# Attention, GLU and routed experts on one core: a new order for the first pass over the GLU's weights

## The chip, the core and the metric

The kernel runs on one core of one Trainium2 chip. Five engines work side by side, each through its own list of instructions in program order: TensorE (PE, matrix products), VectorE (DVE), ScalarE (ACT), GpSimd (POOL) and SyncE (SP), which here only issues DMAs. The tile framework puts semaphores where one engine needs another's result; it does not reorder. An instruction that waits holds back all that stands behind it on its engine. The metric is the device time of one execution in microseconds (us). Execution times come from several runs; the profile is of one execution.

## What is computed

Sizes: 2304 tokens (4 sequences of 576), 8 heads of 64, width 512. A sliding window attention, a GLU with 1536 inner columns and a mixture of eight experts with two per token follow each other.

```python
# attention: position i sees i-63 .. i of its own sequence
scores = scale * q @ k.T;  masked outside the window;  attn = softmax(scores);  x = attn @ v
# GLU; its three weights are float64
gate = 1.0 / (1.0 + np.exp(-(x @ w_gate)))
x = ((gate * (x @ w_val)) @ w_out).astype(np.float32)
# experts
noisy_logits = x @ w_gate2 + np.log1p(np.exp(x @ w_noise)) * noise
top2 = np.argpartition(-noisy_logits, 2, axis=1)[:, :2]      # softmax over the two
for e in range(8):
    out[mask] += top2_w[mask, k, None] * (np.maximum(x[mask] @ w1[e], 0.0) @ w2[e])
```

## The kernel before

Tokens go in 18 tiles of 128; three tiles make a block (384 columns), six blocks a pass each over the GLU's weights (NB = 6). The weights come in twelve words f of 128 inner columns (NF1 = 12), each with three parts: gate, val and out. A product in near single precision is made of three matmuls with split operands, high x high, high x low and low x high (`mm3`, lines 56 to 58).

**A step** is one f of one block: 12 matmuls for gate and 12 for val (128x384, `glu_in`), tanh on ACT (L313), the product on DVE (`mul`, L318), its split into a high half on ACT (`gh`, L325) and a low half on DVE (`low`, L329), and 9 matmuls of 128x512 with the part out of the step before (`out`). One bank each holds gate and val, so the next step's val waits for `mul`.

**Conversion.** The weights arrive as float64, in pairs of 32-bit words, 512 KB for a part. In the first pass each step f also converts word f + 2, in seven instructions on 1536 columns: ACT takes the magnitude from the upper word (`m`, L182) and the rounding from the lower (`r`, L190); DVE shifts (`s`, L195), puts in the sign (`o`, L200) and adds the rounding (`a`, L206); ACT writes the high half (`h`, L214), DVE the low half (`l`, L219) in the step after. The magnitude of word f + 3 is begun in step f. Raw and converted word share one place per f, tag `W{f}`. The magnitude is held by turns in a buffer of its own (`mA`) and in the first half of the place of word 11 (`mB`); the rounding lies in that place's second half. So raw word 11 can only be loaded when word 10 has been rounded. The places of words 8 to 10 hold the queries, keys, values and scores of attention tiles 1 and 2 first; raw 8 to 10 are loaded after steps 1 to 3, raw 11 after step 8.

**Attention** of one tile spreads over four steps: scores (`S`, PE), mask and minimum (`M`, eight custom instructions on DVE, L246), exponential (`E`, ACT, L253), reciprocal (`R`) and normalisation in two halves (`N0`, `N1`, L264) on DVE, transposes in two halves of four (`PT0`, `PT1`, PE, L270), product with v (`O`), split of the result (`X`, L297).

**What sets the order.** The framework keeps the order in which the code is written. For the steps it is given by four strings, ORDER for the first pass and ORDER1 for the others, one string for each of four consecutive steps (f % 4). The prologue, before the steps, is written out by hand: attention of tiles 0 to 2 and the conversion of words 0 and 1. SP's queue takes all loads of that part: qk and v tiles, raw words, the noise (2304 lines of 32 bytes) and an initial fill of the table `slots`.

**Later.** In passes 1 to 5 the routing is worked in; then each of the eight experts gathers up to 640 rows by five indirect DMAs on POOL (L649), and adds its results into the output by five more (L720). `slots` is written by 36 indirect DMAs (L498).

The strings, and the loads that a step may issue:

```python
ORDER = (
    "l r gate M2 E2 s tanh val M3 E3 o mul gh m a low h out",
    "l r gate E4 s tanh val R o mul gh N0 m a low h out N1",
    "PT0 l r gate PT1 s tanh val o mul gh m a low h out",
    "O S X l r gate M0 E0 s tanh val o mul M1 E1 gh m a lv lq low h out",
)
if b == 0 and f in (1, 2, 3, 8):
    load_raw(f + 7 if f < 4 else 11)
```

Of the kernel before, what the change touches and what calls it, by code (L numbers as in the profile page):

```python
# [19 lines left out]
P = 128  # L20
# [25 lines left out]
def build(nc, tc, a, out):  # L46
# [80 lines left out]
    with c1:  # L127
# [6 lines left out]
        def place(f, dt, name):  # L134
# [24 lines left out]
        def load_raw(f, js=range(3)):  # L159
            for i in js:  # L160
                if f < NF1:
                    if f not in WR:
                        r = place(f, I32, "raw")
                        WR[f] = r.rearrange("p (n w) -> p n w", w=2)
                    nc.sync.dma_start(WR[f][:, i * 512:(i + 1) * 512].rearrange("p n w -> p (n w)"),
                                      a["moe_w"].bitcast(I32)[f, i])
# [13 lines left out]
        def cv_m(f, i=W3):  # L180
            if f < NF1:
                nc.scalar.activation(cv_ms(f)[:, cut(i)].bitcast(F32), WR[f][:, cut(i), 1].bitcast(F32), AF.Abs,  # L182
                                     scale=2.0 ** -112)

        def cv_r(f, i=W3):
            if f < NF1:
                if f not in rnd:
                    r = pr.tile([P, 3 * 512], I32, tag="x2", name="rnd")
                    rnd[f] = r
                nc.scalar.activation(rnd[f][:, cut(i)], WR[f][:, cut(i), 0].bitcast(U32), AF.Copy, scale=2.0 ** -29)  # L190

        def cv_s(f, i=W3):
            if f < NF1:
                m = cv_ms(f)[:, cut(i)]
                nc.vector.tensor_scalar(m, m, 3, None, op0=OP.logical_shift_left)  # L195

        def cv_o(f, i=W3):
            if f < NF1:
                m = cv_ms(f)[:, cut(i)]
                nc.vector.scalar_tensor_tensor(m, WR[f][:, cut(i), 1], -2147483648, m, op0=OP.bitwise_and,  # L200
                                               op1=OP.bitwise_or)

        def cv_a(f, i=W3):
            if f < NF1:
                m = cv_ms(f)[:, cut(i)]
                nc.vector.tensor_tensor(m, m, rnd[f][:, cut(i)], op=OP.add)  # L206

        def cv_h(f, i=W3):
            if f < NF1:
                m = cv_ms(f)[:, cut(i)].bitcast(F32).rearrange("p (i c) -> p i c", c=512)  # L210
                if f not in WP:
                    w = place(f, F32R, "W")
                    WP[f] = w.rearrange("p (i a c) -> p i a c", i=3, a=2)
                nc.scalar.activation(WP[f][:, i, 0], m, AF.Copy)  # L214

        def cv_l(f, i=W3):
            if f < NF1:
                m = cv_ms(f)[:, cut(i)].bitcast(F32).rearrange("p (i c) -> p i c", c=512)
                nc.vector.tensor_tensor(WP[f][:, i, 1], m, WP[f][:, i, 0].bitcast(F32), op=OP.subtract)  # L219
# [30 lines left out]
        def attn_E(t, cs):  # L250
            sm, st = Pt[t]
            for c in cs:
# [48 lines left out]
        def glu_in(b, f, i, cols=slice(0, BW), ks=range(NK)):  # L301
# [4 lines left out]
            h, l = WP[f][:, i, 0], WP[f][:, i, 1]  # L306
# [27 lines left out]
        def glu_out(b, f):  # L334
# [3 lines left out]
            h, l = WP[f][:, 2, 0], WP[f][:, 2, 1]  # L338
# [168 lines left out]
        def fill_slots():  # L507
            fill = pr.tile([P, NS, 4], I32, tag="x2", name="fill")
# [18 lines left out]
        for rs in (slice(0, 1), slice(1, 4)):  # L527
            nc.sync.dma_start(qk0[:, rs], a["qk"][0, :, rs])
        load_raw(0, (0,))
        load_vv(0)  # L530
        load_qk(1)
# [4 lines left out]
        load_raw(1)  # L536
        attn_S(0, SB[0])
        load_qk(3)
        load_raw(2)
        attn_M(0, LO)  # L540
        attn_E(0, LO)
        late_consts()
        attn_M(0, HI)
        attn_E(0, range(4, 7))
# [17 lines left out]
        attn_X(0)  # L562
        load_vv(3)
        load_raw(3)
        load_raw(4)
        attn_E(1, HI)
        cv_a(0)
        nrm(1, 0)
        cv_h(0)
        pts(1, 0)  # L570
        attn_M(2, range(8))
        attn_E(2, LO)
# [136 lines left out]
        def y_out(e, j):  # L709
# [42 lines left out]
        )  # L752
        ORDER1 = (
# [250 lines left out]
```

## Time and profile before

| | us |
|---|---|
| median of three runs | 1067.2 (1065.19 to 1068.86) |
| the profiled execution, its own time | 1065.99 |
| its span | 1064.2, at a mean granted clock of 0.985 |
| PE busy | 1007.4 (95%) |
| DVE, ACT, POOL busy | 576.6, 385.6, 153.5 |

The page cuts the span into 40 slices; in the first seven PE is busy for four to eight tenths, after that for nine or more. The first pass ends with the last product out of step 11, which starts at 159.26 us. [...] A wait is listed under the engine that waited, with what came last. In timelines the brackets hold the idle time just ahead of an instruction and its releaser. "DVE early" or "DVE m" is the scratch that the conversion works in.

### The profile page before, as it was taken

What the parts mean: (1) busy time and instruction counts of PE and PEld (TensorE: products, weight loads), DVE (VectorE), ACT (ScalarE), POOL (GpSimd) and SP (SyncE); (2) the same over time, 40 slices, a digit from 0 to 9 for tenths busy, and PEclk for the clock granted to TensorE, in tenths of its full rate; (3) what the DMA queues carried; (4) which work ended last, traced back from release to release, by engine and by line L of the source; (5) the groups of instructions that cost most, each with busy time, mean ns of one, the idle gap of its engine ahead of it and who ended that gap; (6) DMA issues with size and microseconds to landing.
All of it is one profiled execution on the core that took longest, in us unless ns stands there. A gap on an engine that the chain in (4) does not pass through costs nothing.

```text
span 1064.2 us, 16667 instructions
## 1 busy us (share of the span) xinstructions
PE 1007.4 (95%) x6460; PEld 918.2 (86%) x6460; DVE 576.6 (54%) x1594; ACT 385.6 (36%) x868; POOL 153.5 (14%) x210
## 2 busy tenths in 40 slices
PE   4787789999999999999999999999999999999995
PEld 3776679999999999999998889999999999999994
DVE  6788747776766776776333634343434344334331
ACT  5767533223233333332113233233333333333321
POOL 0000000000200200020221224022130505050302
PEclk9988989999999999999999999999999999999998
DMA  9860223222223333342704435434362717262403
GB/s 338 316 260 1 104 85 115 104 94 86 83 102 114 94 108 104 104 108 82 259 2 138 151 119 114 144 73 146 89 170 80 179 59 162 78 158 101 88 2 53
DMA packets 56568, 126.78 MB, mean 119 GB/s; under 512 B 13968, under 2 KB 14112, under 8 KB 56480
## 3 DMA queue, kind: packets, MB, share of 16 engines
q1 hardware_dynamic: 46304, 104.56, 29.0%
q0 software_dynamic: 10176, 21.07, 10.1%
q8 instruction: 53, 0.87, 0.3%
q14 instruction: 35, 0.29, 0.1%
HBM read 101.11 MB, written 24.49 MB: 118 GB/s over the span
## 4 chain that ended last, share of the span: by engine, by line
PE 81%; issue 6%; DVE 4%; DMA 3%; ACT 3%; POOL 1%; SPq 0%; DVEq 0%; ACTq 0%; POOLq 0%
PE gv L56 9%; PE gv L58 9%; PE gv L57 9%; PE hp L57 6%; PE hp L56 6%; PE hp L58 6%; PE yacc L56 6%; PE yacc L57 6%; PE yacc L58 6%; PE acc L56 4%; PE acc L58 4%; PE acc L57 4%; PE PTp L270 2%; PE xgp L662 2%; PE Sp L232 1%
## 5 line engine op out<-in xcount | busy, mean ns | idle before, releaser
L56 PE MATMUL gv<-xT,W 128*128 128x384 f32 (+2 forms) x584 | 204.2, 350 | 3.0 <-ACT th L313 2.3
L57 PE MATMUL gv<-xT,W 128*128 128x384 f32 (+2 forms) x584 | 198.4, 340 | 0.0
L58 PE MATMUL gv<-xT,W 128*128 128x384 f32 (+2 forms) x584 | 198.4, 340 | 0.0
L687 DVE SCALAR_TENSOR_TENSOR hl<-hp,hh 128x320 fp32r<-128x320 f32 (+2 forms) x128 | 62.9, 491 | 198.7 <-ACT hh L686 194.9
L56 PE MATMUL hp<-xgT,h 128*128 128x320 f32 (+2 forms) x512 | 162.3, 317 | 0.0
L58 PE MATMUL hp<-xgT,l 128*128 128x320 f32 (+2 forms) x512 | 159.5, 312 | 0.0
L57 PE MATMUL hp<-xgT,h 128*128 128x320 f32 (+2 forms) x512 | 159.4, 311 | 0.0
L686 ACT ACTIVATE hh<-hp 128x320 fp32r<-128x320 f32 (+2 forms) x128 | 56.0, 438 | 218.7 <-PE hp L58 218.7
L396 DVE CUSTOM_DVE_ANT_0 dump<-x,wb 128x512 bf16<-128x512 f32 x192 | 132.1, 688 | 3.1
L56 PE MATMUL yacc<-h,hh 128*128 128x512 f32 (+1 forms) x328 | 126.9, 387 | 0.0
L57 PE MATMUL yacc<-l,hh 128*128 128x512 f32 (+1 forms) x328 | 126.6, 386 | 0.0
L58 PE MATMUL yacc<-h,hl 128*128 128x512 f32 (+1 forms) x328 | 126.5, 386 | 0.0
L56 PEld LDWEIGHTS gv<-xT,W 128*128 128x128 f32 x584 | 112.0, 192 | 8.9 <-ACT th L313 3.3
L498 POOL DMA_INDIRECT slots<-rec,sli x36 | 39.0, 1084 | 544.3 <-DVE rec L488 455.5
L720 POOL DMA_INDIRECT out<-yo,tb x40 | 66.5, 1662 | 326.7 <-ACT yo L716 318.2
L57 PEld LDWEIGHTS gv<-xT,W 128*128 128x128 f32 x584 | 112.0, 192 | 1.5
L58 PEld LDWEIGHTS gv<-xT,W 128*128 128x128 f32 x584 | 111.8, 191 | 0.0
L318 DVE SCALAR_TENSOR_TENSOR th<-th,gv 128x384 f32<-128x384 f32 x72 | 39.8, 553 | 120.1 <-PE gv L58 94.6
L56 PEld LDWEIGHTS hp<-xgT,h 128*128 128x128 f32 x512 | 96.4, 188 | 2.2 <-DVE hl L687 0.4
L57 PEld LDWEIGHTS hp<-xgT,h 128*128 128x128 f32 x512 | 96.4, 188 | 1.8
L58 PEld LDWEIGHTS hp<-xgT,l 128*128 128x128 f32 x512 | 96.2, 188 | 1.2 <-DVE l L630 0.2
L325 ACT ACTIVATE gH<-th 128x384 fp32r<-128x384 f32 x72 | 37.8, 524 | 135.8 <-DVE th L318 131.3
(143 smaller groups left out, 1572.9 us busy)
## 6 DMA issues: line engine op xcount, KB each, us to landing
raw<-in_moe_w SPq DMA_DIRECT2D x36, 512.0 KB
wb<-in_wgn SPq DMA_DIRECT2D x32, 512.0 KB
r<-in_w SPq DMA_DIRECT2D x32, 512.0 KB
r<-in_moe_w SPq DMA_DIRECT2D x32, 512.0 KB
qk<-in_qk SPq DMA_DIRECT2D x15, 640.0 KB
v<-in_v SPq DMA_DIRECT2D x32, 256.0 KB
out<-zero SPq DMA_DIRECT2D x26, 256.0 KB
xd<-x SPq DMA_DIRECT2D x6, 768.0 KB
```

Of the source, the lines that this page charges most:

```text
L56: nc.tensor.matmul(o, lh, rh, start=start, stop=False)
L57: nc.tensor.matmul(o, lh, rl, start=False, stop=False)
L58: nc.tensor.matmul(o, ll, rh, start=False, stop=stop)
L270: nc.tensor.transpose(p[:, k * P:(k + 1) * P], sm[:, g * 4 + k], ident)
L318: nc.vector.scalar_tensor_tensor(g, g, 1.0, gv.pop(1)[:, :BW], op0=OP.add, op1=OP.mult)
L325: nc.scalar.activation(gh, g, AF.Copy)
L396: nc.vector.tensor_tensor_reduce(out=dump, in0=x2[b][:, j], in1=WB[8 * b + c // 2][:, c % 2], op0=OP.mult, op1=OP.add, scale=1.0, scalar=0 ...
L498: st = nc.gpsimd.indirect_dma_start(out=slots, out_offset=bass.IndirectOffsetOnAxis(ap=sli[:, k, j:j + 1], axis=0), in_=rec[:, j, k, :], i ...
L662: nc.tensor.transpose(p[:, c], xg[:, c], ident)
L686: nc.scalar.activation(hh[:, c], o, AF.Relu)
L687: nc.vector.scalar_tensor_tensor(hl[:, c], o, 0.0, hh[:, c].bitcast(F32), op0=OP.max, op1=OP.subtract)
L720: st = nc.gpsimd.indirect_dma_start(out=out, out_offset=bass.IndirectOffsetOnAxis(ap=tb[:, j, 0:1].bitcast(I32), axis=0), in_=yo, in_offse ...
```

## The change

1. Both magnitude buffers (`ms`) and the rounding (`rnd`) get space of their own, and nothing of the conversion lies in word 11's place any more. The fill of `slots` goes there for the prologue.
2. All raw words 4 to 11 are loaded at the end of the prologue, behind qk 4, the noise and the fill; no step loads one.
3. The order of a step: the shift ahead of `r`, gate and `l`; the attention parts at a step's end or behind val.
4. The prologue: the loads begin in another order, word 0 is converted in three parts with places of their own, the first part ahead of the first tile's mask instructions; the first val follows the first gate sooner; the constants of `late_consts` come first.
5. The exponentials are counted by an upper bound (`attn_E(t, upto)`); the numbers in ORDER1 change with that notation.
6. The scratch for GpSimd's DMA descriptors goes from 8192 to 4096 bytes per partition.

```diff
-        early = {f: place(f, I32 if f == NF1 - 1 else F32, "early") for f in (8, 9, 10, 11)}
+        early = {f: place(f, F32, "early") for f in (8, 9, 10, 11)}
...
-        mA = pc.tile([P, 3 * 512], I32, name="m")
-        mB = part(NF1 - 1, 0, 1536)
-        rnd = {f: part(NF1 - 1, 1536, 1536) for f in range(NF1 - 1)}
-
-        def cv_ms(f):
-            return mB if f % 2 and f < NF1 - 1 else mA
+                if f == 0:
+                    r = place(f, I32, "raw", i)
+                    WR[f, i] = r.rearrange("p (n w) -> p n w", w=2)
+                elif i == 0:
+                    r = place(f, I32, "raw").rearrange("p (n w) -> p n w", w=2)
+                    WR[f] = r
+                    for k in range(3):
+                        WR[f, k] = r[:, k * 512:(k + 1) * 512]
+                nc.sync.dma_start(WR[f, i].rearrange("p n w -> p (n w)"), a["moe_w"].bitcast(I32)[f, i])
...
+        ms = [pc.tile([P, 3 * 512], I32, name=f"m{i}") for i in range(2)]
+        late_consts()
+        rnd = pr.tile([P, 3 * 512], I32, tag="x2", name="rnd")
...
-                if f not in rnd:
-                    r = pr.tile([P, 3 * 512], I32, tag="x2", name="rnd")
-                    rnd[f] = r
-                nc.scalar.activation(rnd[f][:, cut(i)], WR[f][:, cut(i), 0].bitcast(U32), AF.Copy, scale=2.0 ** -29)
+                nc.scalar.activation(rnd[:, cut(i)], raw(f, i, 0).bitcast(U32), AF.Copy, scale=2.0 ** -29)
...
-            fill = pr.tile([P, NS, 4], I32, tag="x2", name="fill")
+            fill = part(NF1 - 1, 0, NS * 4).bitcast(I32).rearrange("p (n w) -> p n w", w=4)
...
+        cv_m(0, C0)
+        cv_r(0, C0)
...
+        cv_s(0, C0)
+        cv_o(0, C0)
+        cv_a(0, C0)
+        attn_M(0, range(8))
+        attn_E(0, 4)
...
+        attn_E(0, 8)
+        attn_M(1, range(8))
+        cv_h(0, C0)
...
-        attn_S(2, SB[2])
-        nc.sync.dma_start(noise, a["moe2_noise"].rearrange("(t p) e -> p t e", p=P))
-        fill_slots()
...
         load_vv(3)
         load_raw(3)
-        load_raw(4)
-        attn_E(1, HI)
-        cv_a(0)
...
+        cv_l(0, C0)
+        cv_s(0, C1)
+        cv_s(0, C2)
+        cv_o(0, C1)
+        cv_o(0, C2)
...
-        glu_in(0, 0, 1, slice(0, 2 * P))
+        attn_M(3, range(4))
         load_qk(4)
-        load_raw(5)
-        load_raw(6)
-        load_raw(7)
-        cv_m(2)
-        attn_M(3, range(4))
-        attn_E(3, range(3))
+        nc.sync.dma_start(noise, a["moe2_noise"].rearrange("(t p) e -> p t e", p=P))
+        fill_slots()
+        for f in range(4, NF1):
+            load_raw(f)
...
         ORDER = (
-            "l r gate M2 E2 s tanh val M3 E3 o mul gh m a low h out",
...
+            "s r gate l tanh val E4 o mul gh a m low h out M2 M3",
...
+            "gate E8 h0 val R N0 tanh mul h1 gh low N1 out h2",
...
-                if b == 0 and f in (1, 2, 3, 8):
-                    load_raw(f + 7 if f < 4 else 11)
...
-    nc = bacc.Bacc("TRN2", target_bir_lowering=False, num_devices=1, dynamic_dma_scratch_size=8192)
+    nc = bacc.Bacc("TRN2", target_bir_lowering=False, num_devices=1, dynamic_dma_scratch_size=4096)
```

The order of the instructions shows it at three places. DVE in step 1, from the last low half ahead of it to the shift behind it (`early` and `m` are the two magnitude buffers before, `m_121` and `m_122` after; `st` and `sm` belong to attention), before:

```order
L219 TENSOR_TENSOR W<-m,W 128x3x512
L195 TENSOR_SCALAR early<-early 128x1536
L258 TENSOR_SCALAR st<-st 128x8
L259 RECIPROCAL st<-st 128x8
L200 SCALAR_TENSOR_TENSOR early<-raw,early 128x1536
L318 SCALAR_TENSOR_TENSOR th<-th,gv 128x384
L264 TENSOR_TENSOR sm<-sm,st 128x512
L206 ISA early<-early 128x3072
L329 TENSOR_TENSOR gL<-th,gH 128x384
L264 TENSOR_TENSOR sm<-sm,st 128x512
L219 TENSOR_TENSOR W<-early,W 128x3x512
```

and after:

```order
L197 TENSOR_SCALAR m_122<-m_122 128x1536
L231 TENSOR_TENSOR W<-m_121,W 128x3x512
L202 SCALAR_TENSOR_TENSOR m_122<-raw,m_122 128x1536
L333 SCALAR_TENSOR_TENSOR th<-th,gv 128x384
L208 ISA m_122<-m_122,rnd 128x3072
L344 TENSOR_TENSOR gL<-th,gH 128x384
L273 TENSOR_SCALAR st<-st 128x8
L274 RECIPROCAL st<-st 128x8
L279 TENSOR_TENSOR sm<-sm,st 128x512 x2
L197 TENSOR_SCALAR m_121<-m_121 128x1536
L231 TENSOR_TENSOR W<-m_122,W 128x3x512
```

The shift (L195, now L197) has changed places with the low half of the word before (L219, now L231), and the two normalisations (L264, now L279) no longer stand around the rounding but behind `low` (L329, now L344).

PE between steps 5 and 6 before, at the first half of the transposes of tile 4 (`acc` is out's product, `gv` gate's or val's):

```order
L57 MATMUL acc<-W,gH 128x512
L58 MATMUL acc<-W,gL 128x512
L270 MATMUL PTp<-ident,sm 128x128 x4
L56 MATMUL gv<-xT,W 128x384
L57 MATMUL gv<-xT,W 128x384
L58 MATMUL gv<-xT,W 128x384
```

and in step 6 after:

```order
L57 MATMUL gv<-xT,W 128x384
L58 MATMUL gv<-xT,W 128x384
L285 MATMUL PTp<-ident,sm 128x128 x4
L56 MATMUL acc<-W,gH 128x512
L57 MATMUL acc<-W,gH 128x512
L58 MATMUL acc<-W,gL 128x512
```

The transposes stood between out of one step and gate of the next; now they stand between val and out of the same step.

SP's queue from the load of raw word 2, before:

```order
L165 DMA raw<-in_moe_w 128x1024 x3
L560 DMA noise<-in_moe_noise 128x18x8
L514 DMA slots<-fill 128x576
L157 DMA v<-in_v 128x512 x2
L165 DMA raw<-in_moe_w 128x1024 x6
L152 DMA qk<-in_qk 128x1280
L165 DMA raw<-in_moe_w 128x1024 x15
L157 DMA v<-in_v 128x512 x2
L152 DMA qk<-in_qk 128x1280
L165 DMA raw<-in_moe_w 128x1024 x3
```

and after:

```order
L171 DMA raw<-in_moe_w 128x1024 x3
L159 DMA v<-in_v 128x512 x2
L171 DMA raw<-in_moe_w 128x1024 x3
L154 DMA qk<-in_qk 128x1280
L620 DMA noise<-in_moe_noise 128x18x8
L529 DMA slots<-early 128x576
L171 DMA raw<-in_moe_w 128x1024 x24
L159 DMA v<-in_v 128x512 x2
L154 DMA qk<-in_qk 128x1280
```

Noise and fill have moved behind raw 3 and qk 4; the 24 loads of words 4 to 11 are one sequence, ahead of the next v and qk.

## Rows read from the trace of the kernel before

**Rows 1.** Table of stretches: start:end, length, busy time of each engine (x instructions), PEclk.

```profile
0.00:44.38 44.38, 24.94 (x293) 21.19 (x294) 29.28 (x102) 28.17 (x72) 2.21 (x16) 1.00 0.87 312
44.38:81.63 37.25, 31.62 (x209) 28.88 (x208) 31.64 (x48) 27.24 (x43) 0.00 (x0) 0.91 0.73 281
81.63:119.06 37.43, 31.81 (x206) 28.60 (x204) 31.63 (x46) 26.25 (x40) 0.00 (x0) 0.91 0.09 32
119.06:132.29 13.23, 7.16 (x35) 5.78 (x33) 7.41 (x13) 4.79 (x9) 0.00 (x0) 0.94 0.32 121
132.29:142.62 10.33, 4.80 (x22) 4.79 (x23) 8.47 (x10) 5.20 (x10) 0.00 (x0) 0.58 0.00 0
142.62:159.26 16.64, 16.64 (x142) 15.33 (x141) 4.69 (x22) 6.03 (x19) 0.00 (x0) 1.00 0.42 135
159.26:400.00 240.74, 240.74 (x1709) 222.12 (x1709) 173.87 (x619) 79.79 (x236) 14.97 (x24) 1.00 0.30 100
```

**Rows 2.** Waits from 44 to 160 us: engine, line, releaser, total us, times, longest.

```profile
PE PTp L270 <- DVE sm L264: 19.8, 3, 10.7
...
PE gv L56 <- ACT th L313: 2.3, 3, 1.3
```

**Rows 3.** Waits of the same stretch, DVE.

```profile
DVE W L219 <- ACT W L214: 8.5, 8, 1.5
```

**Rows 4.** Table of stretches: one at half clock, one with short PE pauses.

```profile
57.10:62.56 5.46, 5.46 (x21) 5.36 (x21) 4.92 (x5) 4.97 (x4) 0.00 (x0) 0.50 1.03 410
...
79.00:91.00 12.00, 9.82 (x47) 7.99 (x46) 10.13 (x16) 9.49 (x18) 0.00 (x0) 1.00 0.00 1
```

**Rows 5.** Waits of SP's queue, 40 to 130 us, then its timeline: start, us, instruction.

```profile
SPq L165 <- DVE m L206: 16.9, 1, 16.9
...
19.81 7.13 SPq L514 DMA_DIRECT2D slots<-fill  x1
...
40.72 0.33 SPq L152 DMA_DIRECT2D qk<-in_qk  x1
...
124.31 1.28 SPq L165 DMA_DIRECT2D raw<-in_moe_w  x3
```

**Rows 6.** Table of stretches: loads alone, last column GB/s.

```profile
56.00:62.00 6.00, 4.90 (x17) 4.80 (x18) 5.46 (x6) 5.26 (x5) 0.00 (x0) 0.50 1.03 410
```

**Rows 7.** Timeline of PE in steps 0 to 2; in brackets idle time before, releaser.

```profile
46.19 0.44 PE L56 MATMUL gv<-xT,W 128*128 128x384 f32 x1 [1.31 <-ACT th L313]
...
50.35 0.34 PE L58 MATMUL gv<-xT,W 128*128 128x384 f32 x1
50.52 0.39 PE L56 MATMUL acc<-W,gH 128*128 128x512 f32 x1
50.75 0.39 PE L57 MATMUL acc<-W,gH 128*128 128x512 f32 x1
...
57.10 1.11 PE L270 MATMUL PTp<-ident,sm 128*128 128x128 f32 x4 [4.33 <-DVE sm L264]
```

**Rows 8.** Timeline of DVE at the end of the prologue.

```profile
42.29 1.75 DVE L219 TENSOR_TENSOR W<-early,W 128x1536 fp32r<-128x1536 f32 x1
...
44.38 0.95 DVE L195 TENSOR_SCALAR m<-m 128x1536 int32<-128x1536 int32 x1
```

**Rows 9.** Chain of waits near 610 us, POOL's timeline, PE's timeline at the gathered rows.

```profile
607.97 4.88 DMA slots<-rec,sli
...
616.07 3.43 DMA xg<-xd,tb
...
661.73 1.01 POOL L649 DMA_INDIRECT xg<-xd,tb  x1 [0.30 <-issue]
663.05 0.98 POOL L649 DMA_INDIRECT xg<-xd,tb  x1 [0.30 <-issue]
...
619.63 0.63 PE L662 MATMUL xgp<-ident,xg 128*128 128x128 f32 x4 [2.34 <-DMA xg<-xd,tb]
...
673.64 0.60 PE L662 MATMUL xgp<-ident,xg 128*128 128x128 f32 x4
```

More of the change, by code (lines that the diff above doesn't have):

```diff
@@ L160, in load_raw, with raw @@
             for i in js:
[L161 to L166, printed above, removed]
-        mA = pc.tile([P, 3 * 512], I32, name="m")
-        mB = part(NF1 - 1, 0, 1536)
-        rnd = {f: part(NF1 - 1, 1536, 1536) for f in range(NF1 - 1)}
-        def cv_ms(f):
-            return mB if f % 2 and f < NF1 - 1 else mA
+                if f == 0:
[7 more added lines that the diff above has]
+                nc.sync.dma_start(WR[f, i].rearrange("p n w -> p (n w)"), a["moe_w"].bitcast(I32)[f, i])
+        def raw(f, i, w):
+            return (WR[f][:, cut(i)] if i.stop - i.start > 1 else WR[f, i.start])[:, :, w]
+        ms = [pc.tile([P, 3 * 512], I32, name=f"m{i}") for i in range(2)]
+        late_consts()
+        rnd = pr.tile([P, 3 * 512], I32, tag="x2", name="rnd")
         def cut(i):
@@ L181, in cv_m @@
             if f < NF1:
-                nc.scalar.activation(cv_ms(f)[:, cut(i)].bitcast(F32), WR[f][:, cut(i), 1].bitcast(F32), AF.Abs,
+                nc.scalar.activation(ms[f % 2][:, cut(i)].bitcast(F32), raw(f, i, 1).bitcast(F32), AF.Abs,
                                      scale=2.0 ** -112)
@@ L198, in cv_o @@
             if f < NF1:
[L199 to L200 removed]
+                m = ms[f % 2][:, cut(i)]
+                nc.vector.scalar_tensor_tensor(m, raw(f, i, 1), -2147483648, m, op0=OP.bitwise_and,
                                                op1=OP.bitwise_or)
@@ L204, in cv_a @@
             if f < NF1:
-                m = cv_ms(f)[:, cut(i)]
-                nc.vector.tensor_tensor(m, m, rnd[f][:, cut(i)], op=OP.add)
+                m = ms[f % 2][:, cut(i)]
+                nc.vector.tensor_tensor(m, m, rnd[:, cut(i)], op=OP.add)
         def cv_h(f, i=W3):
             if f < NF1:
-                m = cv_ms(f)[:, cut(i)].bitcast(F32).rearrange("p (i c) -> p i c", c=512)
-                if f not in WP:
+                m = ms[f % 2][:, cut(i)].bitcast(F32).rearrange("p (i c) -> p i c", c=512)
+                if f == 0:
+                    w = place(f, F32R, "W", i.start)
+                    WP[f, i.start] = w.rearrange("p (a c) -> p a c", a=2)
+                    nc.scalar.activation(WP[f, i.start][:, 0], m[:, 0], AF.Copy)
+                else:
                     w = place(f, F32R, "W")
                     WP[f] = w.rearrange("p (i a c) -> p i a c", i=3, a=2)
-                nc.scalar.activation(WP[f][:, i, 0], m, AF.Copy)
+                    for k in range(3):
+                        WP[f, k] = WP[f][:, k]
+                    nc.scalar.activation(WP[f][:, :, 0], m, AF.Copy)
         def cv_l(f, i=W3):
             if f < NF1:
-                m = cv_ms(f)[:, cut(i)].bitcast(F32).rearrange("p (i c) -> p i c", c=512)
-                nc.vector.tensor_tensor(WP[f][:, i, 1], m, WP[f][:, i, 0].bitcast(F32), op=OP.subtract)
+                m = ms[f % 2][:, cut(i)].bitcast(F32).rearrange("p (i c) -> p i c", c=512)
+                if f == 0:
+                    w = WP[f, i.start]
+                    nc.vector.tensor_tensor(w[:, 1], m[:, 0], w[:, 0].bitcast(F32), op=OP.subtract)
+                else:
+                    nc.vector.tensor_tensor(WP[f][:, :, 1], m, WP[f][:, :, 0].bitcast(F32), op=OP.subtract)
         xT = {}
@@ L248, in attn_M, with attn_E @@
                                                accum_out=st[:, 0, c:c + 1])
-        def attn_E(t, cs):
+        En = {}
+        def attn_E(t, upto):
             sm, st = Pt[t]
-            for c in cs:
+            n, En[t] = En.get(t, 0), upto
+            for c in range(n, upto):
                 nc.scalar.activation(sm[:, c], sm[:, c], AF.Exp, bias=st[:, 0, c:c + 1], scale=-1.0,
@@ L525, in pts @@
             attn_PT(t, g, ("OP", "acc2")[g])
-        for rs in (slice(0, 1), slice(1, 4)):
-            nc.sync.dma_start(qk0[:, rs], a["qk"][0, :, rs])
+        C0, C1, C2 = (slice(i, i + 1) for i in range(3))
+        nc.sync.dma_start(qk0[:, 0:1], a["qk"][0, :, 0:1])
         load_raw(0, (0,))
+        nc.sync.dma_start(qk0[:, 1:4], a["qk"][0, :, 1:4])
+        load_qk(1)
         load_vv(0)
-        load_qk(1)
         load_raw(0, (1, 2))
@@ L796, in build @@
                     acts[f"M{i}"] = lambda i=i: ta < TT and attn_M(ta, range(2 * i, 2 * i + 2))
-                for i, cs in enumerate(ES):
-                    acts[f"E{i}"] = lambda cs=cs: ta < TT and attn_E(ta, cs)
+                for i in range(1, 9):
+                    acts[f"E{i}"] = lambda i=i: ta < TT and attn_E(ta, i)
                 for i in range(3):
```

62 lines of the change are left out of this document (31 added, 31 removed), and 11 rows, old and new, of tables (ORDER, ORDER1).

## Prediction

> **What bounds the kernel now.** I read the table of stretches first, cut where VectorE (DVE) starts the shift of words 2, 6, 10 and 11, where it ends the last conversion (142.62) and where TensorE (PE) starts the last product of the first pass (159.26) [rows 1]. From 142.62 to 400 PE is busy all the time: what reaches 159.26 earlier moves the rest of the program up by as much. From 44.38 to 142.62 it is not. Four steps take 37.25 and 37.43 us, in which PE and DVE are each busy about 31.6, and the next two stretches take 23.56 us with 11.96 of PE. PE's waits from 44 to 160 us are 19.8 us in three waits of the transposes (PTp) for the normalisation on DVE, the longest 10.7, and 2.3 at step entries for tanh [rows 2]. In the same steps DVE waits for ScalarE (ACT), 8.5 us in 8 waits of the low half (L219) for the high half (L214) [rows 3]. So PE and DVE wait for each other in turn, and neither is full. The long waits have a second price: PE runs at half its clock behind them, at 0.50 for 5.46 us after the first [rows 4]. Over the four stretches busy time by missing clock is 31.62 x 0.09 + 31.81 x 0.09 + 7.16 x 0.06 + 4.80 x 0.42 = 8.2 us [rows 1]. The 10.7 us wait begins as a wait for a load: SP held raw word 11 back for 16.9 us, until DVE had added word 10's rounding, and issued it at 124.31 [rows 5].
>
> **The loads of words 4 to 11 (gain).** Rounding and the second mantissa buffer leave the space of W11, so raw 11 goes out with all others at the prologue's end. A word of 1.5 MB takes 3.8 us at 410 GB/s [rows 6], all eight 31; a word is used every 31.6 / 4 = 7.9 us. Once raw 4 is there the loads gain 4 us on each word. SP's wait goes, and what it caused. What would be late next is DVE.
>
> **The order in the steps (gain).** On DVE the shift goes ahead of the low half, which gives ACT's high half another 0.9 us, and no wait stands in its place as long as ACT keeps up: it is busy 27.24 and 26.25 per four steps [rows 1], over 4 us less than DVE. N0 and N1 go to the end of their step, ahead of the next step's conversion, and PT0 behind val instead of ahead of gate: 24 matmuls lie between normalisation and use, so I cost PTp's first two waits at nothing, and the half clock behind them. If that cover is gone, the wait has the size it has now, 4.33 us at 57.10 [rows 7]. Late next is DVE again: four steps of the same instructions keep it busy 31.63, PE without its half clock 31.62 - 2.85 = 28.8 and 31.81 - 2.86 = 28.9. ORDER1, for the later passes, issues the same work in the same places.
>
> **The prologue (near nothing).** Before, DVE starts the low half of word 1 at 42.29, does two mask instructions and shifts word 2 at 44.38 [rows 8]; after, the shift is ahead of these 2.09 us. The marker moves to 42.3, and the work behind it grows by as much. Word 0 in thirds adds 8 instructions to DVE and 6 to ACT for the same work; DVE is busy 29.28 and ACT 28.17 of 44.38 us [rows 1], so there are 15 idle us to hide their fixed parts, unless they fall on the chain from the first load to the first gate. No row shows a 128x512 conversion. A third of the low half's 1.75 us [rows 8] is 0.6: I bound the prologue by -2 us (three such instructions of head start) and +2 (0.25 for each of DVE's 8, somewhat more than the 0.17 that is left for a mask instruction in those 2.09 us), and take 0, as idle time is the larger. Two fill instructions of DVE now stand here; their input comes from GpSimd, busy 2.21 of 44.38 us, long before.
>
> **SP's queue (a risk, counted at nothing).** Noise and fill now stand ahead of raw 4 instead of v3 and raw 3. The fill held SP 7.13 us, and the qk load ahead of them went out at 40.72 [rows 5]. From there 40.7 + 0.4 + 7.1 = 48.2 for raw 4's issue, 3.8 for its bytes and about 1 to land: 53. Shift 2 starts at 42.3 and shift 4 two steps on, at 42.3 + 2 x 7.9 = 58.1, with the 1.6 us of ACT's magnitude ahead: it is wanted at 56.5. Nothing waits, with 3.5 us to spare; raw 5 has 7. Behind all loads queue v4 and qk 5: in at 48 + 31 + 2 = 81, wanted in step 7, at 42.3 + 7 x 7.9 = 97.6.
>
> **The sum** is made against the profiled run: its time 1065.99 is 1.2 below the median of 1067.2. From shift 2 to the last low half DVE has 31.64 + 31.63 + 7.41 + 8.47 of work [rows 1] and the 2.09 moved behind the marker, 81.2 us. It starts at 42.3 and without gaps ends at 123.5, not 142.62: 19.1 less. Then came 16.64 us of PE. In these PE did val of step 10 and out for word 9 first, 12 x 0.17 + 9 x 0.23 = 4.1 us by the starts of such matmuls [rows 7]; they need nothing of word 11, and PE, with 2.8 us of slack in four steps, will have done them. That leaves 12.5. I take 13.5, 1.0 for a restart behind DVE and ACT as at 46.19, where PE stood 1.31 us [rows 7], and keep 16.64 as the upper end. So 3.1 more, 22.2 in all. The other way round: 22.1 of waits and 8.2 of half clock are 30.3 that PE could get back at most, less DVE's excess over PE, 31.63 - 28.85 = 2.8 in each of 81.2 / 31.63 = 2.57 periods, 7.1: 23.2. I take 22: the profiled run becomes 1065.99 - 22 = 1044, the median 1067.2 - 22 = **1045**. With 3.1 for the tail, 2 for the prologue either way and the other sum's 1: 1042 to 1049.
>
> **Rivals.**
> 1. PE is the bound: DVE's busy time counts tails which overlap in a full stream, its 31.6 shrinks towards PE's 28.9, and up to the 7.1 come back: 1038 to 1041. For it: its busy time is taken from stretches with gaps, where nothing overlaps a tail. Against: the whole 2.8 of four steps would have to be tails. 7 in 100.
> 2. The clock falls all the same. PE, ahead of DVE, waits about 1 us several times in four steps. For it: half clock stands behind the long waits. Against: from 79 to 91 us PE was busy only 9.82 of 12 us at granted 1.00 [rows 4]. Price: 5.46 us at half clock lose 2.7; one such dip in four steps hides in DVE's excess of 2.8, a second doesn't and costs 2.57 x 2.7 = 7, a third 14: 1052 to 1059. 12 in 100. [...]
> 3. Raw 4 is late: noise and fill hold SP longer than 7.13 + 3.5 us, now that a longer queue is ahead of them. ACT, DVE and PE then wait once, in step 1, for the excess. For it: the 7.13 itself, against: later words catch up 4 us each. At 3 to 6 us in excess 1048 to 1051. 8 in 100.
> 4. Slower than before, by GpSimd's DMAs. The change halves the space for their descriptors. If one must then wait until an earlier one has landed, they start 3.4 to 4.9 us apart, the time a gather and a scatter take to land, where now it is 1.3 [rows 9]. The six scatters up to 607.97 lead to expert 0's gather, for which PE already waits 2.34 us: 5 x 3.6 = 18 us. In each later expert five adds and five gathers go in a row; the first gather, at 661.73, lands at 665.2 and is used at 673.64, so 8.5 us are covered. With 2 us more for each of the six up to it 3.5 are not, 25 in seven experts: 18 + 25 - 22 = +21, about 1088. It is slower from about 2 us more per DMA on. Against: no row of before shows a wait for such space. 4 in 100. [...]
> 5. The change does only half of what it says: PT1, now behind out, and tanh and val in their new places make PE wait as often as before, and only word 11's load is won: 10.7 of the waits and 2.0 of the half clock, 1067.2 - 12.7 = 1054.5. Against: nothing stands between N1 and PT1 that needs DVE to be late. 3 in 100, 1 of it for a gain under 3 us.
>
> **How the numbers follow.** The forecast of 1045 has 66 in 100, rivals 1 to 5 have 7, 12, 8, 4 and 3. The range 1040 to 1054 leaves out rival 4, half of rival 1, two thirds of rival 2 and rival 5: 4 + 3.5 + 8 + 3, under 20. 0.3%, 3 us, is what a measurement of this kernel can tell from no change: faster by more 0.95, within it 0.01, slower by more 0.04.
>
> **What would show it.** Right: the three long waits of PTp and SP's wait for word 10 are gone; the granted clock is 1.00 from 45 to 137; from shift 2 to 6 and 6 to 10 it is 31.5 to 32.5 us, with DVE busy nearly all of it and PE idle 2 to 3; the last low half ends near 123.5, word 11's product starts near 137, and from there to the end it is 905 us as before (1064.2 - 159.26). Wrong on the order if DVE waits over 3 us in four steps, on the clock if a stretch reads 0.50, on SP if ACT waits for raw 4, on GpSimd if the 905 us grow.

## The result

The changed kernel takes 1049.26 us, the median of four runs (1047.7 to 1050.29); the kernel before, with one run more, 1067.79. The ratio is 0.9829, with an interval from 0.9806 to 0.9851: 18.5 us faster, where 22 were forecast. The time lies in the stated range. The profiled execution is the slowest of the four, 1050.29 us with a span of 1048.5, so against the profiled one of before 15.7 us are to be found in the traces.

The table of stretches of the changed kernel, cut at the same events as [rows 1] (start of shifts 2, 6 and 10, end of the last low half, first product of word 11); columns are start and end, length, busy time of PE, PEld, DVE, ACT and POOL with numbers of instructions, granted clock of TensorE as a share of full speed, DMA share, GB/s:

```profile
0.00:44.89 44.89, 24.73 (x284) 20.50 (x285) 28.02 (x106) 25.79 (x71) 2.11 (x16) 1.00 0.66 248
44.89:76.66 31.77, 27.36 (x200) 24.09 (x200) 31.29 (x47) 26.46 (x40) 0.00 (x0) 1.00 1.02 386
76.66:108.39 31.73, 29.31 (x206) 25.98 (x205) 31.25 (x48) 25.94 (x40) 0.00 (x0) 1.00 0.31 116
108.39:126.25 17.86, 16.94 (x89) 15.01 (x88) 17.79 (x28) 13.63 (x28) 0.00 (x0) 1.00 0.01 2
126.25:139.91 13.66, 13.66 (x129) 12.63 (x127) 4.42 (x21) 5.54 (x18) 0.00 (x0) 1.00 0.46 144
139.91:1048.50 908.59, 893.79 (x5562) 816.10 (x5561) 463.36 (x1360) 288.11 (x680) 151.52 (x194) 0.99 0.37 108
```

Four steps take 31.75 us instead of 37.3; VectorE is busy in 31.29 and 31.25 of them. The granted clock reads 1.00 from shift 2 to the first product of word 11, and the pace agrees: the matmuls of 128x384 start 0.17 to 0.18 us apart there, where at 0.50 [rows 4] they start 0.32 apart. (For the prologue the reading does not hold, see experiments 6 to 8.) That product starts at 139.91 instead of 159.26, 19.35 us earlier. The rest of the program, the same instructions, takes 908.59 us where it took 904.94, and gives 3.65 of them back. The waits from 40 to 150 us (engine, line, what came last, total, times, longest), which answer [rows 2] and [rows 3]:

```profile
PE Op L302 <- ACT pt L287: 3.1, 2, 1.6
PE PTp L285 <- DVE sm L279: 2.6, 3, 0.9
PE gv L56 <- ACT th L328: 2.1, 2, 1.3
...
DVE W L231 <- ACT W L222: 0.8, 2, 0.4
```

PE's 19.8 us for the normalisation are 2.6 now, VectorE's 8.5 us for the high half 0.8. SP's queue, which had to hold raw word 11 back [rows 5], runs through:

```profile
43.35 0.33 SPq L154 DMA_DIRECT2D qk<-in_qk  x1
43.72 0.43 SPq L620 DMA_DIRECT2D noise<-in_moe_noise  x1
45.05 2.09 SPq L529 DMA_DIRECT2D slots<-early  x1
47.19 24.50 SPq L171 DMA_DIRECT2D raw<-in_moe_w  x24
```

### The profile page after: what moved, and what is told of

Its sections match the earlier page's. It is cut to its first block, busy times and chain, and to the rows that moved or that the text cites. A ratio compares the mean times of both kernels' runs of the same rounds, so it can differ in the third digit from the quotient of the medians.

```text
span 1048.5 us, 16688 instructions
## 1 busy us (share of the span) xinstructions
PE 1005.8 (96%) x6460; PEld 914.3 (87%) x6460; DVE 576.1 (55%) x1602; ACT 385.5 (37%) x874; POOL 153.6 (15%) x210
## 4 chain that ended last, share of the span: by engine, by line
PE 81%; issue 5%; DVE 5%; DMA 4%; ACT 2%; POOL 1%; SPq 0%; DVEq 0%; POOLq 0%; ACTq 0%
PE gv L56 9%; PE gv L57 8%; PE gv L58 8%; PE hp L58 6%; PE hp L56 6%; PE hp L57 6%; PE yacc L56 6%; PE yacc L57 6%; PE yacc L58 6%; PE acc L56 4%; PE acc L58 4%; PE acc L57 4%; DMA raw<-in_moe_w 2%; PE PTp L285 2%; PE Op L302 2%
## 5 line engine op out<-in xcount | busy, mean ns | idle before, releaser
L56 PEld LDWEIGHTS gv<-xT,W 128*128 128x128 f32 x584 | 110.7, 189 | 10.7 <-ACT th L328 3.3
L57 PEld LDWEIGHTS gv<-xT,W 128*128 128x128 f32 x584 | 110.7, 189 | 2.4 <-DVE xT L312 0.7
L58 PEld LDWEIGHTS gv<-xT,W 128*128 128x128 f32 x584 | 110.6, 189 | 0.0
L56 PE MATMUL acc<-W,gH 128*128 128x512 f32 x216 | 86.6, 401 | 0.0
```

The source lines that it names most:

```text
L56: nc.tensor.matmul(o, lh, rh, start=start, stop=False)
L57: nc.tensor.matmul(o, lh, rl, start=False, stop=False)
L58: nc.tensor.matmul(o, ll, rh, start=False, stop=stop)
```

## The experiments

My theory was that of the forecast, with two additions from the trace above: the steps are bound by VectorE; the early loads alone are worth a few us and the order of the steps most of the gain; what is missing went into the new prologue (2.6 us) and into the clock after 139.91 (3.65 us). The rivals were the early loads as the whole gain, a chain of waits between engines as the bound of the steps, and GpSimd's smaller descriptor space as the place where the missing part went. Ratios are to runs of the kernel before on the same chip.

### 1. The old order in the changed kernel

```diff
-            "s r gate l tanh val E4 o mul gh a m low h out M2 M3",
-            "s r gate l tanh val E8 o mul gh a m low h out R N0 N1",
-            "s r gate l tanh val PT0 o mul gh a m low h out PT1",
-            "s r gate l tanh val O S o mul X gh a m low h out lv lq M0 M1",
+            "l r gate M2 E5 s tanh val M3 E6 o mul gh m a low h out",
+            "l r gate E8 s tanh val R o mul gh N0 m a low h out N1",
+            "PT0 l r gate PT1 s tanh val o mul gh m a low h out",
+            "O S X l r gate M0 E2 s tanh val o mul M1 E3 gh m a lv lq low h out",
```

> The changed kernel with the step order of before (the four strings of ORDER; own buffers, early loads and the new prologue stay). My theory, that the order removes two of the three long waits of PTp and the half clock behind them: both waits return at 4 to 5 us each with half clock behind them, four steps take 36.5 to 37.5 us instead of 31.8, the first product of word 11 starts near 152 instead of 139.9, the time is about 1061 (1058 to 1064). The rival, that nearly all of the gain is the early load of word 11: four steps stay under 33 us and the time within 2 us of the changed kernel's 1049.3.

Measured: 1065.25 us, ratio 0.9979 (0.9967 to 0.9991). Its table of stretches from shift 2 to 6 and 6 to 10, and its waits of PE for the normalisation:

```profile
47.21:84.20 36.99, 31.71 (x204) 28.86 (x204) 31.54 (x48) 27.12 (x46) 0.00 (x0) 0.91 0.97 379
84.20:121.14 36.94, 30.66 (x204) 27.54 (x204) 31.55 (x46) 26.15 (x40) 0.00 (x0) 0.95 0.11 33
```

```profile
PE PTp L285 <- DVE sm L279: 12.5, 3, 4.8
```

The waits of up to 4.8 us, the lower clock (0.91 and 0.95) and the 37 us per four steps are back, with all weights loaded early. So the order is what turns 37 into 31.75 us: with everything else as changed it is worth 1065.25 - 1049.26 = 16.0 us. The time is a us above my range, and two thirds of the expected saving over the kernel before are missing: shift 2 starts only at 47.21, against 44.38 in the kernel before with the same order, which pointed at the prologue. What each single move in the strings gives was not tried, nor the new order without the early loads.

### 2. Only the buffers and loads

In the kernel before, with the smaller descriptor space that makes the room:

```diff
-        mB = part(NF1 - 1, 0, 1536)
-        rnd = {f: part(NF1 - 1, 1536, 1536) for f in range(NF1 - 1)}
+        mB = pc.tile([P, 3 * 512], I32, name="mb")
+        rnd0 = pr.tile([P, 3 * 512], I32, tag="x2", name="rnd")
+        rnd = {f: rnd0 for f in range(NF1)}
...
-        load_raw(7)
+        for f in range(7, NF1):
+            load_raw(f)
...
-                if b == 0 and f in (1, 2, 3, 8):
-                    load_raw(f + 7 if f < 4 else 11)
...
```

> The kernel before with own buffers for magnitude and rounding and the loads of words 4 to 11 issued by the end of the prologue; step order and prologue as before. My theory: only the third wait of PTp shrinks, from 10.7 to 4 to 5 us, four steps stay at 37.3 us, SP no longer waits for word 10, the first product of word 11 starts near 152 and the time is 1060 (1058 to 1062). The rival, that the loads are all of it: 1049 to 1053.

Measured: 1061.88 us, ratio 0.9957 (0.9943 to 0.9971). The stretch from shift 10 (118.68) to the end of the last low half, and the wait of PE:

```profile
118.68:136.31 17.63, 11.67 (x54) 10.61 (x54) 15.70 (x22) 9.71 (x17) 0.00 (x0) 0.81 0.00 1
```

```profile
PE PTp L271 <- DVE sm L265: 12.4, 3, 4.8
```

17.63 us, where the kernel before took 13.23 + 10.33 = 23.56 [rows 1]: the load costs 5.9 us, not the 10.7 of its wait, because a wait of 4.8 stands in the same place without it. The loads alone give 5.3 us by the medians, between a quarter and a third of the 18.5. With the old order and the early loads, the old prologue is 3.4 us better than the new one (1061.88 against 1065.25).

### 3. The smaller descriptor space alone

```diff
-    nc = bacc.Bacc("TRN2", target_bir_lowering=False, num_devices=1, dynamic_dma_scratch_size=8192)
+    nc = bacc.Bacc("TRN2", target_bir_lowering=False, num_devices=1, dynamic_dma_scratch_size=4096)
```

> The kernel before with 4096 instead of 8192 bytes for GpSimd's DMA descriptors and nothing else. My theory: no change, 1067.8 give or take 2; the indirect DMAs of the experts last 0.95 and 1.56 us as before and PE waits 2.3 us once for a gather. The rival (the space is too small, and part of the missing 3.5 us of gain goes there): POOL's DMAs grow by 0.3 us or more and the time by over 3 us.

Measured: 1066.91 us, ratio 0.9994 (0.9980 to 1.0008). The groups of POOL's instructions, with busy time and mean ns of one, first here, then in the kernel before:

```profile
L720 POOL DMA_INDIRECT out<-yo,tb x40 | 66.3, 1658 | 328.3 <-ACT yo L716 319.8 <-issue 6.6 <-DVE hl L687 1.8
...
L649 POOL DMA_INDIRECT xg<-xd,tb x40 | 38.8, 971 | 17.1 <-issue 9.9 <-PE acc L58 4.4 <-PE hp L58 1.5
```

```profile
L720 POOL DMA_INDIRECT out<-yo,tb x40 | 66.5, 1662 | 326.7 <-ACT yo L716 318.2 <-issue 6.6 <-DVE hl L687 1.8
...
L649 POOL DMA_INDIRECT xg<-xd,tb x40 | 38.9, 972 | 16.9 <-issue 11.1 <-PE acc L58 4.2 <-PE hp L58 1.5
```

None of POOL's DMA instructions is longer (the third group, the writes of `slots`, has a mean of 1084 ns in both), and the time is the same. This rival has fallen.

### 4. VectorE relieved

The sign is left out in the parts val and out of words 2 to 11:

```diff
         def cv_o(f, i=W3):
             if f < NF1:
+                i = slice(0, 1) if f > 1 else i
...
```

> The changed kernel, with the sign put only into the gate's part of words 2 to 11 (512 instead of 1536 columns; the signs of val's and out's weights are left out). It takes 1.1 us of VectorE out of each step and nothing else. My theory, that VectorE bounds the steps: four steps fall from 31.75 us to TensorE's 28.5 to 29.5, the first product of word 11 starts 6 to 9 us earlier, the time is about 1042 (1040 to 1044). The rival, that a chain of waits from engine to engine bounds the steps and VectorE only looks full: four steps shorten by less than 1 us and the time by less than 2.

Measured: 1040.61 us, ratio 0.9762 (0.9741 to 0.9784). Shift 2 to 6 and 6 to 10:

```profile
44.34:72.12 27.78, 26.00 (x195) 23.38 (x195) 27.21 (x45) 26.15 (x40) 0.00 (x0) 1.00 1.02 383
72.12:100.02 27.90, 27.90 (x203) 25.72 (x202) 27.17 (x46) 25.81 (x40) 0.00 (x0) 1.00 0.48 177
```

VectorE is busy 4.1 us less in four steps (27.21 and 27.17 instead of 31.29 and 31.25); they shorten by 4.0 and 3.8 us, and the whole by 8.65. VectorE is the bound of the changed steps. In the second stretch TensorE is busy all of 27.90 us: there the next bound begins, 0.6 us below the 28.5 to 29.5 that I had given.

### 5. The prologue of before under the new order

Word 0 whole again, attention and loads in the old order, the new strings.

```diff
-        cv_m(0, C0)
-        cv_r(0, C0)
...
-        cv_m(0, C1)
-        cv_m(0, C2)
+        cv_m(0)
...
-        attn_E(2, 4)
-        attn_X(1)
-        cv_s(1)
-        cv_r(1)
-        glu_in(0, 0, 0, slice(0, 2 * P))
-        nrm(2, 0)
+        attn_E(2, 6)
+        cv_s(1)
+        attn_X(1)
+        nrm(2, 0)
...
```

> The new step order, own buffers and early loads, with the prologue of before (word 0 converted whole, attention and loads in the old order; raw 8 to 11 issued at its end). My theory, that the new prologue costs what is missing from the forecast: shift 2 starts at 42 to 42.5 instead of 44.9, four steps take 31.7 us, the first product of word 11 starts at 136.5 to 137.5, the time is 1046 (1045 to 1047.5), 3 us below the changed kernel. The rival, that the later start is a matter of the step order (it moves work behind the marker) and not of the prologue: shift 2 near 44.5 and the time within 1 us of 1049.3.

Measured: 1045.17 us, ratio 0.9792 (0.9778 to 0.9806). Its stretches from shift 2 on:

```profile
41.81:73.55 31.74, 28.19 (x208) 24.94 (x208) 31.26 (x46) 25.60 (x39) 0.00 (x0) 1.00 1.01 399
73.55:105.29 31.74, 29.30 (x206) 25.97 (x205) 31.26 (x46) 26.00 (x40) 0.00 (x0) 1.00 0.13 40
```

Shift 2 starts at 41.81, and the steps behind it are those of the changed kernel. This is the time that the forecast gave for the changed kernel: the prologue is where the forecast was too good, and this version is 4 us faster than the changed kernel and 23 faster than the kernel before.

### 6, 7 and 8. What in the prologue

The trace of the changed kernel shows this chain at tile 1's result and the first gate, on ACT (the split, L311, behind the magnitude of word 1 and four exponentials, of which the first stands here), PE and VectorE:

```profile
30.48 1.58 ACT L187 ACTIVATE m<-raw 128x1536 f32<-128x1536 f32 x1
31.97 0.39 ACT L268 ACTIVATE early<-early,st 128x128 f32<-128x128 f32 x1
...
33.51 0.57 ACT L311 ACTIVATE xT<-Op 128x512 fp32r<-128x512 f32 x1
```

```profile
34.13 0.58 PE L56 MATMUL gv<-xT,W 128*128 128x256 f32 x1 [2.28 <-ACT xT L311]
```

```profile
34.12 0.69 DVE L312 TENSOR_TENSOR xT<-Op,xT 128x512 fp32r<-128x512 f32 x1 [4.20 <-ACT xT L311]
```

VectorE stands 4.20 us for the split, with shift 1 and tile 2's normalisation behind the waiting instruction; PE stands 2.28 us, with the transposes of tile 2 behind the gate. Three kernels undo parts of it. The seventh has the first of these edits alone, the eighth the second alone. The sixth has both and, beyond them, tile 2's last four exponentials ahead of word 1's rounding on ACT, so the seventh and the eighth do not add up to it:

```diff
-        attn_E(2, 4)
         attn_X(1)
+        attn_E(2, 4)
```

```diff
-        glu_in(0, 0, 0, slice(0, 2 * P))
         nrm(2, 0)
         cv_o(1)
         attn_E(2, 8)
         pts(2, 0)
-        glu_in(0, 0, 1, slice(0, 2 * P))
+        glu_in(0, 0, 0, slice(0, 2 * P))
...
         attn_X(2)
+        glu_in(0, 0, 1, slice(0, 2 * P))
```

> The changed kernel with three edits in its prologue: the split of tile 1 (X) ahead of tile 2's exponentials, the first half of tile 2's transposes ahead of the first gate, and the first val behind the scores of tile 3. My theory, that in the new prologue PE stands for tile 1's split (2.28 us) with tile 2's transposes queued behind the gate: shift 2 starts 1.2 to 2.5 us earlier than 44.9, the time is 1047 to 1048. The rival, that the late scores of tile 0 (8.65 instead of 6.94 us, its load queues behind word 0's first part) run through the whole prologue: shift 2 stays within 0.5 us of 44.9.

> One of the three prologue edits alone: tile 1's split (X) on ACT ahead of tile 2's first four exponentials, the rest as changed. If the exponentials ahead of the split are the cause of PE's 2.28 us wait for the first gate, that wait falls to under 1 us, shift 2 starts at 43.0 to 43.6 instead of 44.9 and the time falls by 1.3 to 1.9. If the gate and val ahead of tile 2's transposes are the cause, shift 2 stays within 0.5 us of 44.9.

> The other two prologue edits alone: tile 2's first transposes ahead of the first gate, the first val behind tile 3's scores; the split stays behind the exponentials. If gate and val ahead of tile 2's transposes are the cause of the late prologue (their 24 matmuls start 0.21 us apart there, twice their later 0.11), shift 2 starts at 42.5 to 43.5 instead of 44.9. If the late split alone is the cause, it stays within 0.5 us of 44.9.

Measured: both 1046.14 us (0.9802, 0.9787 to 0.9817), the split first 1046.88 (0.9802, 0.9778 to 0.9825), the transposes first 1049.09 (0.9818, 0.9792 to 0.9845). Shift 2 on VectorE starts at 41.96 with both, 43.44 with the split first, 46.12 with the transposes first:

```profile
41.96 0.95 DVE L197 TENSOR_SCALAR m<-m 128x1536 int32<-128x1536 int32 x1
```

```profile
43.44 0.95 DVE L197 TENSOR_SCALAR m<-m 128x1536 int32<-128x1536 int32 x1
```

```profile
46.12 0.95 DVE L197 TENSOR_SCALAR m<-m 128x1536 int32<-128x1536 int32 x1
```

The second parts of word 0, whose loads come early in the prologue, are shifted at 17.70, 19.61 and 19.59 in these three and at 18.77 in the changed kernel, so part of the differences was there before the place of the edits. From that shift to shift 2 it is 24.3 us with both, 23.8 with the split first, 26.5 with the transposes first and 26.1 in the changed kernel. Experiments 4 and 9, with the prologue of the changed kernel, have 26.2 and 25.2, so such a figure moves by a us from one execution to the next. The split behind the exponentials costs about 2 us: 2.3 from the shift on, 2.4 by the medians, and every run of the seventh kernel is faster than every run of the changed one. PE's wait for the first gate falls to 0.75 us, as expected, and the time falls by more than the expected 1.3 to 1.9. As long as the split is late, nothing is gained by the transposes ahead of the gate: they then wait themselves, 4.97 us for the exponentials, and shift 2 at 46.12 lies outside both of the ranges that I had given.

The price is more than the wait. Behind it the matmuls of the first gate and of half of the first val run at half pace in the changed kernel (first two lines); in the seventh they run at full pace (second two):

```profile
35.46 0.41 PE L56 MATMUL gv<-xT,W 128*128 128x256 f32 x1
35.67 0.41 PE L57 MATMUL gv<-xT,W 128*128 128x256 f32 x1
```

```profile
34.52 0.28 PE L57 MATMUL gv<-xT,W 128*128 128x256 f32 x1
34.64 0.28 PE L58 MATMUL gv<-xT,W 128*128 128x256 f32 x1
```

They start 0.21 us apart instead of 0.12. The granted clock reads 1.00 here in the trace of the changed kernel, which this pace contradicts; in the trace of the ninth kernel, with the same prologue, it reads 0.50 where the matmuls start 0.21 apart (34.66 to 37.85 us). In the old prologue (experiment 5) the first gate runs at that pace too (0.21 us apart from 34.30 on), but not val (0.12 apart from 40.13 on).

Between the sixth kernel and the old prologue 1 us remains in the median, between the seventh and the old prologue 1.7. Half a us of it may be the two instructions of the fill on VectorE, which in the changed kernel stand directly ahead of shift 2, from 44.35 to 44.89, with no idle time before them. What word 0 in thirds makes of it, or the later scores of tile 0 (PE started them at 7.05 instead of 5.35), was not tried alone; all this stays open.

### 9 and 10. GpSimd for a third of the low halves

```diff
-                    nc.vector.tensor_tensor(WP[f][:, :, 1], m, WP[f][:, :, 0].bitcast(F32), op=OP.subtract)
+                    for e, k in ((nc.vector, slice(0, 2)), (nc.gpsimd, slice(2, 3))) if f > 1 else ((nc.vector, W3),):
+                        e.tensor_tensor(WP[f][:, k, 1], m[:, k], WP[f][:, k, 0].bitcast(F32), op=OP.subtract)
```

The ninth kernel is the changed one with this, the tenth that of experiment 5.

> The changed kernel with the low half of the part out (512 of 1536 columns) of words 2 to 11 on GpSimd, which does nothing in the first pass. If VectorE bounds the steps: its 0.56 us less per step bring four steps from 31.75 to 29.5 us and the time to about 1043.5 (1042 to 1045), as long as GpSimd needs under 5 us for it. The rival, that the two engines get in each other's way: VectorE's instructions beside it grow by 10% or more and the time stays within 2 us of 1049.3.

> The prologue of before, the new steps and the low half of the part out on GpSimd together. If the two gains are on the same path one after the other they add: 3 us and 5.8 us, 1040.5 (1039 to 1042). If TensorE becomes the bound of the steps, the second gain is cut: 1042 to 1044.

Measured: 1052.59 us (0.9861, 0.9844 to 0.9878) and 1050.72 (0.9836, 0.9819 to 0.9854), both slower than without it, by 3.3 and 5.6 us. GpSimd's instruction and VectorE's beside it in the ninth kernel:

```profile
60.07 1.41 POOL L232 TENSOR_TENSOR W<-m,W 128x512 fp32r<-128x512 f32 x1 [6.75 <-ACT W L222]
69.10 2.32 POOL L232 TENSOR_TENSOR W<-m,W 128x512 fp32r<-128x512 f32 x1 [7.62 <-ACT W L222]
```

```profile
60.24 2.07 DVE L197 TENSOR_SCALAR m<-m 128x1536 int32<-128x1536 int32 x1
62.23 1.21 DVE L232 TENSOR_TENSOR W<-m,W 128x1024 fp32r<-128x1024 f32 x1
...
70.20 2.84 DVE L202 SCALAR_TENSOR_TENSOR m<-raw,m 128x1536 int32<-128x1536 int32 x1
```

The shift takes 2.07 us instead of 0.95 beside a subtraction of 1.41 on GpSimd, the sign 2.84 instead of 1.75. VectorE loses 1.1 us to save 0.56. The growth that the rival named came, at a higher price than the 2 us that it allowed, and the forecasts of 1043.5 and 1040.5 were wrong.

### 11. The normalisation on ACT

On the kernel of experiment 5, for tiles 3 to 5:

```diff
-            nc.vector.tensor_tensor(sm[:, c], sm[:, c], st[:, 2, c, None].to_broadcast([P, 4, P]), op=OP.mult)
+            if 3 <= t <= 5:
+                for k in range(g * 4, g * 4 + 4):
+                    nc.scalar.activation(sm[:, k], sm[:, k], AF.Copy, scale=st[:, 2, k:k + 1])
+            else:
+                nc.vector.tensor_tensor(sm[:, c], sm[:, c], st[:, 2, c, None].to_broadcast([P, 4, P]), op=OP.mult)
```

> The prologue of before, the new steps, and the normalisation of tiles 3 to 5 on ACT (eight multiplications of 128x128 by a column) instead of VectorE. It takes 1.2 us of VectorE out of four steps. If VectorE still bounds them and ACT, with 5 us of slack in four steps, can take it: four steps fall from 31.7 to 30.5 to 31.0 and the time from 1045.2 to 1042 to 1044. The rival, that ACT's 2.3 us in one step delay tanh and with it VectorE's next products: no gain, 1045 to 1046.

Measured: 1045.94 us (0.9792, 0.9770 to 0.9814), no gain over 1045.17. ACT first, then VectorE:

```profile
57.90 2.44 ACT L270 ACTIVATE sm<-sm,st 128x128 f32<-128x128 f32 x8
60.24 1.63 ACT L191 ACTIVATE rnd<-raw 128x1536 int32<-128x1536 uint32 x1
61.78 0.47 ACT L321 ACTIVATE th<-gv 128x384 f32<-128x384 f32 x1
```

```profile
62.28 0.56 DVE L326 SCALAR_TENSOR_TENSOR th<-th,gv 128x384 f32<-128x384 f32 x1 [0.80 <-ACT th L321]
```

The eight multiplications stand ahead of rounding and tanh, VectorE waits 0.80 us for tanh, and what it was spared it spends waiting: the steps from shift 2 (42.14) to shift 6 (73.72) and to shift 10 (105.25) take 31.58 and 31.53 us, and it is busy 30.40 of 31.86 us from 42.14 to 74.00 and 30.56 of 32.00 from there to 106.00. The granted clock is 0.95 in the first of these two stretches but 1.00 in the second, so the clock is not the reason. ACT has slack over four steps, but not in that one.

## Why the forecast was right, and where it was not

**The steps, right.** From shift 2 to the end of the last low half I had 81.2 us; it is 126.25 - 44.89 = 81.4. From there to word 11's product I had 13.5; it is 13.66. That both meet to 0.2 us is partly luck. VectorE is busy 80.33 of the 81.4 us, 0.9 less than I had summed, and idles the 1.0 that I had put at nothing; and the 1.0 for a restart behind VectorE did not come, since PE is busy for all 13.66 us: in its place stand the end of out for word 9 and four transposes. Experiment 4 shows that VectorE is the bound, as the sum supposed, and experiments 1 and 2 that the order takes PTp's waits of up to 4.8 us away and the loads the excess of the third. The clock stayed at 1.00 although PE still idles 2.4 to 4.4 us in four steps: rival 2 did not come in the changed kernel. One dip of rival 2's kind came in the seventh kernel: behind a wait of 1.25 us for tanh in step 0, PE's matmuls start 0.32 us apart from 46.68 on, and the granted clock is 0.95 over the first four steps. Behind the same wait of 1.25 us the changed kernel runs on at full pace (0.17 to 0.18 us apart). The dip, 3.4 us long where the forecast had counted with 5.46, cost nothing, as the forecast said of a single one: from shift 2 to word 11's product it is 95.04 us there and 95.02 in the changed kernel.

**The prologue, wrong.** The step of the sum that failed is the term for the prologue: "take 0, as idle time is the larger". Shift 2 starts at 44.89, not 42.3, 2.6 us late and beyond my bound of 2. (Experiments 4 and 9, with the same prologue, have 44.34 and 43.54; experiments 5, 10 and 11, with the old one, 41.81, 42.74 and 42.14: 2.0 us less in the mean.) I had counted the added instructions and their idle cover, and the head start on VectorE, but had not followed who waits for whom in the new sequence: that the exponentials of tile 2 came ahead of the split of tile 1 on ACT, that PE stands 2.28 us for it, and that the matmuls behind the wait run at half pace (0.21 us apart instead of 0.12). I had asked whether the fill's instructions would wait, but not counted the 0.54 us that they take. With the old prologue (experiment 5) shift 2 starts at 41.81 and the median is 1045.17, against a forecast of 1045.

**The rest of the program, wrong by the clock.** "From there to the end it is 905 us as before" was 908.59 in the profiled run. GpSimd is not the reason (experiment 3). The granted clock shows two places. First ten us each of the changed kernel, from the routing's narrow matmuls (128x16) on and from the first gather of expert 0 on:

```profile
564.94:574.94 10.00, 10.00 (x50) 8.50 (x49) 7.58 (x27) 3.50 (x7) 0.00 (x0) 0.83 0.75 288
602.46:612.46 10.00, 10.00 (x51) 8.63 (x51) 2.42 (x6) 1.91 (x4) 3.39 (x5) 0.83 0.69 226
```

The same of the kernel before:

```profile
584.75:594.75 10.00, 10.00 (x54) 8.46 (x54) 8.63 (x38) 3.08 (x8) 0.00 (x0) 1.00 0.68 260
619.63:629.63 10.00, 10.00 (x62) 8.86 (x63) 2.71 (x7) 2.24 (x6) 3.18 (x5) 1.00 0.71 230
```

0.17 of ten us twice are 3.4, and PE waited 2.73 instead of 2.34 us for the gather: 3.8 for the missing 3.65. PE's busy time agrees: 893.79 us in the changed kernel, and in the kernel before, from 159.26 on (six stretches summed),

```profile
sum 904.94, PE 890.40 PEld 813.63 DVE 463.46 ACT 287.94 POOL 151.26; mean PE 148.40 PEld 135.60 DVE 77.24 ACT 47.99 POOL 25.21
```

so 3.4 of the 3.65 are slower work and not waits. It is not the change that does this. Experiment 3, with the instructions of before, has 0.83 behind the gather too:

```profile
620.27:630.27 10.00, 10.00 (x51) 8.59 (x51) 2.42 (x6) 1.91 (x4) 3.18 (x5) 0.83 0.70 229
```

Of all 13 profiles the kernel before is the only one with 1.00 there, so the profile that I calculated from was the unusual one. In the profiles of the experiments, counted in the same way, the rest takes between 905.9 and 908.0 us: the 904.94 are the lowest of all, and the 908.59 of the changed kernel the highest. By the medians only 3.5 us are missing from the forecast in all, 2.0 to 2.6 of them in the prologue, so most of the 3.65 is a matter of which executions were profiled.

**Balance** of the profiled runs: 22.2 (which I had rounded to 22) - 2.6 (prologue) - 0.2 - 0.2 (steps and tail) - 3.65 (rest) = 15.55, measured 15.7. One sum of the prediction is off by a us: 1045 with 3.1 for the tail and 2 for the prologue gives 1050 as its upper end, not 1049.

**Loads of words 4 to 11 and SP's queue.** The risk that raw 4 comes late did not come true: the fill held SP 2.09 instead of 7.13 us in its new place. For the about 1 us of landing I had named no row; in the trace of before raw 11's last bytes move until 130.0 and ACT starts on them at 130.67. My 10.7 + 2.0 for the loads alone in rival 5 were more than twice too much: experiment 2 gives 5.3 us by the medians.

## What to carry to other kernels

Two engines that are each busy for 85% and wait in turn can be brought to the bound of one by their order, once the loads do not stand in the way; what is left is the busy time of the longer one, nearly unbroken: 80.3 of 81.4 us here. A moved prologue has to be followed instruction by instruction on each queue, since one split behind four short instructions cost about 2 us that no busy share shows. The granted clock is best read together with the pace of the matmuls: in one stretch here it read 1.00 where they ran at half pace, 0.21 us apart instead of 0.12. Before work is moved off the bound, look whether the helper holds the bound up (GpSimd, beside which VectorE's shift took 2.07 instead of 0.95 us) or has its slack in another place (ACT, for whose tanh VectorE waited 0.80 us).

## What the runs showed of the hardware

- VectorE was slower beside GpSimd: with a 128x512 subtraction on GpSimd (1.41 to 2.32 us in the first four steps of experiment 9), one of VectorE's instructions in each step grew by 1.1 us. The shift took 2.07 us and the sign 2.84 in experiment 9, 2.06 and 2.85 in experiment 10, against 0.95 and 1.75 in the changed kernel.
- Behind PE's wait for the first gather, 1.97 to 3.13 us long, the granted clock over the next ten us was 0.70 to 0.86 in twelve of 13 profiles and 1.00 in one: 1.00 behind 2.34 us in the kernel before, 0.83 behind 2.28 in experiment 3, with the same instructions.
- 24 narrow matmuls (128x16), busy for 2.88 us, were followed by 0.83 over ten us in the changed kernel and in experiment 10, and by 1.00 in the eleven others.
